# The causal mask of the first query block: a matmul with an identity, or an add inside the masked maximum

## The chip, the cores and the metric

The kernel runs on one core of a Trainium2 chip. The metric is the device time in microseconds (us) of one execution. Three runs of the kernel before took 554.1, 554.99 and 555.74 us; the median is 554.99 us. The engines are called PE (TensorE: matmuls; PEld is its weight load), DVE (VectorE), ACT (ScalarE), POOL (GpSimd) and SP (SyncE, which issues most DMAs).

## The reference, cut to what matters

The program mixes two branches by a gate: an attention with a compressive memory over four segments of 512 tokens, 16 heads of 28, and a feed-forward network (448 to 1792 to 448 with SiLU).

```python
for s in range(N):                       # 4 segments, L = 512
    qs, ks, vs = q[:, :, s], k[:, :, s], v[:, :, s]
    logits = einsum("bhqd,bhkd->bhqk", qs, ks) * scale + mask      # mask: -1e9 above the diagonal
    p = softmax(logits)
    a_dot = einsum("bhqk,bhkd->bhqd", p, vs)
    num = einsum("bhld,bhde->bhle", phi(qs), M)
    den = einsum("bhld,bhd->bhl", phi(qs), z)[..., None] + 1e-6
    o = g * num / den + (1 - g) * a_dot
    M, z = M + einsum("bhld,bhle->bhde", phi(ks), vs), z + phi(ks).sum(l)
a = concat(o) @ wo
b = silu(x @ w1) @ w2
out = gate * a + (1 - gate) * b          # gate = sigmoid(sum(x * gate_w))
```

What the change touches is the maximum of each row of `logits`, which the softmax needs before the exponentials, under the causal mask.

## The kernel before, in words

**Precision.** Operands of matmuls are split in two fp16 halves, so most products are three passes; a product over 448 rows is 11 matmuls (L616).

**Work.** There are 16 groups `t`: 4 segments times 4 groups of 4 heads. For each group the kernel projects q and k, retrieves from the memory, and then:

- `maxima(t, o)` computes the row maxima. Scores are made for query blocks of 128 rows (`i` = 0 to 3) against 128 x (i+1) keys, in PSUM banks of the ring "sc" (three banks of 512 columns). The plan is: block 0 for four heads in one bank, block 1 for two heads at a time, blocks 2 and 3 for one head at a time. For `i > 0` DVE makes one pass per head: it adds the mask from the tile `MK` and takes the maximum (L731, a masked maximum with an accumulator that is read out into `mx`). `MK` is 512 columns wide, zero but for its last 128, which hold the causal triangle; `MK[:, L - n:]` serves every block. For `i == 0` one matmul first writes the triangle into the bank for all four heads (L717: identity times `maskb`, 512 columns), the four score matmuls add to it (L721), and one plain reduce of 512 columns gives four maxima (L726). Then the maxima are lifted (L739), transposed on PE (L741), split in halves (L743, L745) and sent as two more rows of the group's q operand by two small DMAs.
- `attention(t)` makes the transposed scores with these rows (L1293), exponentials on ACT (L1298), the causal zeros on POOL (L1301, L1304), halves on ACT and POOL (L1310, L1314), the product with v (L1327), a reduce on DVE (L1335), the scaling on POOL (L1343, L1344) and a store.
- `ffn(i, ...)` runs the feed-forward network in two passes over its 14 blocks; its first product is L616, its second L1197, and tanh, products and halves between them lie on ACT and DVE (L1174 to L1180). It fills PE between the steps of the attention.
- `last_part` runs in the last stage: it loads the attention's output `o` and the memory's share, adds them on POOL (L627), makes halves (L633, L583), transposes by DMA (L641), multiplies by wo (L616 with `oT`), and adds the feed-forward part (L1404, L1408).

**The order.** Nothing of this order is written out by hand. Every step is a task with a modelled cost, dependencies, buffers of rings and a priority, and `Sched.run` (L221) lists them: at each turn it takes the engine whose best task can start first by the modelled costs; among tasks of an engine that can start at the same moment the lower priority number goes first, and for PE `matmuls` (L210) adds PRICE times a measure of uncovered weight loads. Each engine, and the DMA queue of SP, then executes its tasks in that order. So any changed cost or priority can redraw the whole order. The cost of a DVE task is 0.07 us + 0.00104 us per column (L328). Constants at the head of the file (L34 to L91) set the priorities: MAXO how early maxima come, FLO and FHI the span of the feed-forward's priorities in the first pass, WOP and WOT how far output projections, their loads and their features stand from the feed-forward work of their block, PVP and LOP those of the product with v and of the low halves, SLACK when an elementwise step goes to the other engine.

**The start.** PE begins with matmuls on the zeroed tile `maskb`: 8 in one task (L797, WARM) and MORE more in a chain at the low priority 200 (L802), which fill the time until the first weights and x have come. When the last of them is done, POOL writes the triangle into `maskb` (L818), as it has before into `MK` (L816); both selects are in `MKS`, for which every group's maxima wait.

```python
for _ in range(MORE):
    END1.append(pe(half(L), lambda: nc.tensor.matmul(
        wb.v, maskb, maskb[:, None, :].to_broadcast([128, 4, 128]), start=True, stop=True),
        END1[-1], uses=[wb], prio=200))
t_wb = END1[-1]
```

Of the kernel before, what the change touches and what calls it, by code (L numbers as in the profile page):

```python
# [14 lines left out]
OP = mybir.AluOpType  # L15
# [18 lines left out]
NA = 5  # L34
COLD = 5.0
WARM = 8
MORE = 34
HPRIO = -62.95
BANKS = {"mm": 3, "sc": 3, "cc": 2}
FREE = FB - 1  # L40
PASSES = [list(range(0, 10)), list(range(10, FB))]
# [3 lines left out]
DOWN = 2.0 ** -19  # L45
TINY = 2.0 ** -40
FIT = 2.0 ** -15
WOT = 71.68
TUS = 1.6
TLAT = 4.0  # L50
SLACK = -0.05
LOP = 28.11
LATE = 0.06
FIRST = 114.09
WPRIO = 110.43
MAXO = 61.39
FULL = 0.111
LOCK = 0.06
RB = "cc"
MP = 24.55  # L60
VF = 0.36
VA = 7.02
VS = 10.8
NV = 8
XH0 = -20.97
WQS = -0.58
VH = -12.56
XS0 = -18.17
VC = -7.5
OT1 = -4.94  # L70
XS = 8.61
QS = -10.12
KS1 = 3.46
SS = -19.24


def VP(o, k):
    return o + VA + VS * k if o or k > VF else -1.0 + 0.1 * k


PRICE = 135.04
PVRUNS = [((1, 0), 1)]
PVP = 21.83
FLO = -2.23
FHI = 720.62
WOP = 1.45
SZ = 35.49
SZSTEP = 1.68
XPRIO = -25.01
WBP = 7.24  # L90
XLEAD = 146.82  # L91


# [179 lines left out]
def infini_mix(ctx: ExitStack, tc: tile.TileContext, x, wq, wk, wv, wo, beta, w1, w2, out):  # L273
# [40 lines left out]
    def half(cols, n=1):  # L314
        return [(0.0025 + cols * 0.000418, 0.027)] * n

    def pe(seq, fn, *deps, **k):
        t = sch.add("PE", sum(max(a[0], b[1]) for a, b in zip(seq, seq[1:])) + seq[-1][0], fn, deps, **k)
        t.lead, t.tail = seq[0][1], seq[-1][0]
        return t  # L320
# [376 lines left out]
    def maxima(t, o):  # L697
# [12 lines left out]
        for q, (i, hs) in enumerate(plan):  # L710
            ps = Buf(BK["sc"])
            n = 128 * (i + 1)
            p0 = o - MAXO + 40 * q / len(plan)

            def go(i=i, hs=hs, ps=ps, n=n):
                if i == 0:
                    nc.tensor.matmul(ps.v, identb, maskb[:, None, :].to_broadcast([128, 4, 128]), start=True,  # L717
                                     stop=False, skip_group_check=True)
                for j, hh in enumerate(hs):
                    u = j * n  # L720
                    nc.tensor.matmul(ps.v[:, u:u + n], rg.v[:KS, 0, hh, i * 128:(i + 1) * 128], rg.v[:KS, 1, hh, :n],  # L721
                                     start=(i > 0), stop=(i > 0 or j == 3), skip_group_check=(i == 0))

            def red(i=i, hs=hs, ps=ps, n=n):
                if i == 0:
                    nc.vector.tensor_reduce(mx.v[:, :, 0], ps.v.rearrange("p (h n) -> p h n", h=4), axis=AX.X,  # L726
                                            op=OP.max)
                    return
                for j, hh in enumerate(hs):
                    r = ps.v[:, j * n:(j + 1) * n]  # L730
                    nc.vector.tensor_tensor_reduce(r, r, MK[:, L - n:], 1.0, NEG, OP.add, OP.max,  # L731
                                                   mx.v[:, hh, i:i + 1])
            m = pe((half(512) if i == 0 else []) + half(n, len(hs)), go, *rs, *MKS, takes=[ps], uses=[rg], prio=p0)
            reds.append(dve(len(hs) * (n + 45) - 45 if i else 512, red, m, *reds[:1], takes=[] if reds else [mx], uses=[ps, mx],
                            prio=p0))
        pt, mh = Buf(BK["sc"]), Buf(C["mhl2"])
        p0 = o - 20
# [14 lines left out]
    def project():  # L752
# [58 lines left out]
        def guards():  # L811
            for j in guard:
# [2 lines left out]
        t_mz = dve(L, lambda: nc.vector.memset(MK, 0.0), prio=-50)  # L815
        MKS.append(pool(128, lambda: nc.gpsimd.affine_select(MK[:, 384:], MK[:, 384:], [[-1, 128]], OP.is_ge, NEG,  # L816
                                                             base=0, channel_multiplier=1), t_mz, prio=-50))
        MKS.append(pool(128, lambda: nc.gpsimd.affine_select(maskb, maskb, [[-1, 128]], OP.is_ge, NEG, base=0,  # L818
                                                             channel_multiplier=1), t_wb, t_mb, prio=-50))
        ONE.append(dma(16e3, lambda: start(onescr.rearrange("a h (b n) -> (a h b) n", b=16), ones[:, :32]), t_on,  # L820
                       prio=50))

# [660 lines left out]
```

## Time and profile before

| | before |
|---|---|
| median of 3 runs | 554.99 us |
| the profiled execution's own time | 555.17 us |
| its span, first to last instruction | 553.1 us |
| PE busy | 540.6 us (98%) |
| DVE busy | 404.9 us (73%) |
| ACT busy | 392.6 us (71%) |
| POOL busy | 345.7 us (63%) |
| DMA, mean over the span | 143 GB/s |

How to read it: a time of the profile is inside the span; the own time of the execution is 2.07 us longer. Matmuls are pipelined, so a matmul's duration overlaps the next one's, and the distance of starts tells what one costs a busy PE. Rows of groups give the line, engine, operation, what is written and read (buffer numbers left out), count, busy time, mean ns of one, and the idle time of the engine just before with what ended it. Rows of the timeline give start, length, engine, line, operation and count, and in brackets an idle time before. Idle time of an engine that is not the bound costs nothing.

### The profile page before, as it was taken

The page shows a single profiled execution, that of the slowest core. Times are in us where ns is not written, and L with a number is a line of the kernel's source. Part 1 is how long each engine was busy: PE and PEld are TensorE (multiplying, and loading weights), DVE is VectorE, ACT ScalarE, POOL GpSimd, SP SyncE. Part 2 cuts the span into 40 slices and gives each one's busy share as a digit, 9 for nine tenths or more (in the row PEclk, how much of TensorE's full clock was granted, in tenths as well). Part 3 has the DMA queues.
Part 4 walks back from the last instruction along what each step waited for, and adds up shares of the span by engine and source line. Part 5 has one row for each costly group of instructions (what it writes and reads, how often), then busy time and mean ns, then how long its engine had stood idle before and what let it go on. Part 6 is the DMA issues. An engine that isn't in the chain of part 4 may idle for free.

```text
span 553.1 us, 11692 instructions
## 1 busy us (share of the span) xinstructions
PE 540.6 (98%) x4084; PEld 301.8 (55%) x4084; DVE 404.9 (73%) x1009; ACT 392.6 (71%) x694; POOL 345.7 (63%) x556
## 2 busy tenths in 40 slices
PE   8899999999999999999999999999999999999987
PEld 3445556656544555555565555555556554555534
DVE  5996999978779964788666889757895149653472
ACT  5887978866557978899787798878997897401140
POOL 3115535756424888899989898888978995212210
PEclk9999999999999999999999999999999999999999
DMA  8687557554567424224232243665200213698872
GB/s 305 202 263 229 189 172 213 162 165 143 178 181 202 122 74 146 71 70 106 70 115 84 70 125 102 136 147 162 55 24 32 85 35 95 219 230 234 224 187 84
DMA packets 78059, 78.94 MB, mean 143 GB/s; under 512 B 44040, under 2 KB 67720, under 8 KB 78000
## 3 DMA queue, kind: packets, MB, share of 16 engines
q1 hardware_dynamic: 77424, 77.21, 48.7%
q10 hardware_dynamic: 576, 0.99, 0.6%
q8 instruction: 32, 0.52, 0.4%
q14 instruction: 27, 0.22, 0.1%
HBM read 48.41 MB, written 26.09 MB: 135 GB/s over the span
## 4 chain that ended last, share of the span: by engine, by line
PE 72%; DVE 11%; DMA 8%; POOL 3%; SPq 2%; issue 2%; ACT 2%; DVEq 0%; POOLq 0%; ACTq 0%
PE mm L616 22%; PE mm L1197 15%; PE sc L1293 6%; PE sc L721 6%; PE cc L1327 6%; PE sc L616 5%; PE cc L1197 4%; PE cc L616 4%; DMA ol<-o_scr 3%; DMA rawf<-in_w_dram 3%; DVE sc L731 2%; DVE xh L583 1%; DMA xraw<-in_x_dram 1%; POOL ol L627 1%; SPq L641 1%
## 5 line engine op out<-in xcount | busy, mean ns | idle before, releaser
L1314 POOL TENSOR_TENSOR phl<-pf,phl 128x384 f16<-128x384 f32 (+1 forms) x192 | 189.7, 1010 | 21.3 <-ACT phl L1310 21.2
L731 DVE CUSTOM_DVE_ANT_0 sc<-sc,mk 128x384 f32<-128x384 f32 (+1 forms) x192 | 105.3, 571 | 30.1 <-PE sc L721 28.6
L1298 ACT ACTIVATE pf<-sc,es 128x512 f32<-128x512 f32 (+1 forms) x192 | 109.5, 618 | 25.1 <-PE sc L1293 22.8
L1197 PE MATMUL mm<-wb,ghl 128*128 128x448 f16 (+1 forms) x516 | 112.6, 348 | 0.0
L616 PE MATMUL mm<-xh,wa 128*128 128x512 f16 x429 | 106.3, 378 | 0.0
L1197 PEld LDWEIGHTS <-ghl 128*128 128x128 f16 x684 | 64.8, 97 | 54.4 <-DVE ghl L1180 2.2
L1310 ACT ACTIVATE phl<-pf 128x1280 f16<-128x1280 f32 x64 | 81.3, 1272 | 11.7 <-POOL pf L1304 11.5
L616 PEld LDWEIGHTS <-wa 128*128 128x128 f16 x572 | 54.4, 97 | 56.5 <-issue 2.6
L1293 PE MATMUL sc<-ring 86*128 86x512 f16 (+3 forms) x256 | 58.6, 299 | 1.3 <-DVE mx L726 1.0
L721 PE MATMUL sc<-ring 84*128 84x128 f16 (+3 forms) x256 | 57.3, 299 | 0.1
L1327 PEld LDWEIGHTS <-phl 128*128 128x128 f16 x1280 | 42.0, 96 | 10.4
L1335 DVE TENSOR_REDUCE oraw<-cc 128x116 f32<-128x232 f32 x64 | 25.3, 395 | 30.0 <-PE cc L1327 29.9
L627 POOL TENSOR_TENSOR ol<-ol,ml 128x448 f32<-128x448 f32 x12 | 13.6, 1133 | 48.5 <-DMA ol<-o_scr 36.3
L1327 PE MATMUL cc<-vg,phl 128*128 128x29 f16 (+1 forms) x1280 | 43.6, 182 | 0.0
L616 PE MATMUL mm<-xh,wqs 128*128 128x512 f16 x176 | 43.1, 379 | 0.0
L616 PE MATMUL mm<-xh,wks 128*128 128x512 f16 x176 | 42.1, 379 | 0.0
L1197 PE MATMUL cc<-wb,ghl 128*128 128x448 f16 x168 | 37.9, 352 | 2.0 <-DVE ghl L1180 1.3
L616 PE MATMUL sc<-wvs,xh 128*128 128x450 f16 x176 | 37.5, 353 | 1.6 <-DVE wvs L583 1.1
L633 ACT ACTIVATE oh<-ol,os 128x448 f16<-128x448 f32 x16 | 10.7, 666 | 39.8 <-POOL ol L627 39.8
L616 PE MATMUL cc<-xh,wa 128*128 128x512 f16 x143 | 37.2, 378 | 0.8 <-DVE amr L1055 0.8
L1293 PEld LDWEIGHTS <-ring 86*128 86x128 f16 x256 | 24.2, 97 | 21.7 <-issue 0.3
L616 PE MATMUL sc<-wos,oT 128*128 128x448 f16 x176 | 35.7, 352 | 0.0
(183 smaller groups left out, 933.7 us busy)
## 6 DMA issues: line engine op xcount, KB each, us to landing
rawf<-in_w_dram SPq DMA_DIRECT2D x26, 256.0 KB
rawf<-in_w_dram SPq DMA_DIRECT2D x28, 224.0 KB
v_scr<-vt SPq DMA_DIRECT2D x16, 232.0 KB
vg<-v_scr SPq DMA_DIRECT2D x16, 232.0 KB
xraw<-in_x_dram SPq DMA_DIRECT2D x14, 256.0 KB
q_scr<-stg SPq DMA_DIRECT2D x16, 224.0 KB
ring<-q_scr SPq DMA_DIRECT2D x16, 224.0 KB
k_scr<-stg SPq DMA_DIRECT2D x16, 224.0 KB
```

The lines of the kernel that those rows point to most:

```text
L616: nc.tensor.matmul(ps(), *p[i], start=(i == 0), stop=(i == n - 1))
L627: d = pool(530, lambda: nc.gpsimd.tensor_add(b.v, b.v, m.v), d, e, uses=[b, m], **k)
L633: hi = copy(D + 110, lambda: nc.scalar.activation(half2.v[:, :D], ol.v, AF.Copy, scale=sc), *ready, takes=[half2], uses=[ol], prio=prio)
L721: nc.tensor.matmul(ps.v[:, u:u + n], rg.v[:KS, 0, hh, i * 128:(i + 1) * 128], rg.v[:KS, 1, hh, :n], start=(i > 0), stop=(i > 0 or j == 3), ...
L731: nc.vector.tensor_tensor_reduce(r, r, MK[:, L - n:], 1.0, NEG, OP.add, OP.max, mx.v[:, hh, i:i + 1])
L1197: nc.tensor.matmul(ps.v[:, lo:hi], g.v[:, y, sl], w.v[:, z, lo:hi], start=(j == 0 and i == 0), stop=(j == len(fs) - 1 and i == 2))
L1293: nc.tensor.matmul(ps.v[:, e:e + w], rg.v[:KK, 1, hh, j * 128:(j + 1) * 128], rg.v[:KK, 0, hh, j * 128:], start=True, stop=True)
L1298: ex.append(sact(e, lambda b=b, ps=ps, pf=pf, e=e: nc.scalar.activation(pf.v[:, b, :e], ps.v[:, :e], AF.Exp, scale=es[:, s:s + 1]), m, *ex ...
L1310: hi = copy(1280, lambda hl=hl, flat=flat: nc.scalar.activation(hl.v[:, 0], flat(), AF.Copy), *mk, takes=[hl], uses=[pf], prio=p0 + 2)
L1314: low = pool(w - u + 22, lambda hl=hl, flat=flat, u=u, w=w: nc.gpsimd.tensor_sub(hl.v[:, 1, u:w], flat()[:, u:w], hl.v[:, 0, u:w]), low, u ...
L1327: nc.tensor.matmul(p[:, i, :2 - z], hl.v[:, z, u:u + 128], vg.v[:, j, hh, :2 - z], start=(z == zs[0] and i == 0), stop=(z == zs[-1] and j ...
L1335: nc.vector.tensor_reduce(orw.v[:, hh], p, axis=AX.X, op=OP.add)
```

## The change

For the first query block of each group the mask matmul (L717) and the reduce over four heads (L726) go. The block is treated like the others: four score matmuls, each with a start of its own, and four masked maxima of 128 columns, one a head, that add the triangle from the last 128 columns of `MK`. The planner's cost of this DVE task goes from 512 columns to 4 x 173 - 45 + 140 = 787, and that of the PE task loses one matmul of 512 columns. The triangle is no longer written into `maskb`, and `MKS` has one entry. MORE goes from 34 to 20 warm-up matmuls. Some thirty constants have other values, so that the planner draws another order.

```diff
@@ -34,8 +34,8 @@
-MORE = 34
-HPRIO = -62.95
+MORE = 20
+HPRIO = -74.28
@@ -45,49 +45,49 @@
-WOT = 71.68
+WOT = 48.81
...
-SLACK = -0.05
-LOP = 28.11
-LATE = 0.06
-FIRST = 114.09
-WPRIO = 110.43
+SLACK = 0.36
+LOP = 26.49
+LATE = 0.04
+FIRST = 108.19
+WPRIO = 114.09
...
-MP = 24.55
-VF = 0.36
-VA = 7.02
-VS = 10.8
+MP = 25.11
+VF = 0.19
+VA = 6.82
+VS = 10.57
...
-XH0 = -20.97
-WQS = -0.58
-VH = -12.56
-XS0 = -18.17
+XH0 = -22.77
+WQS = -0.68
+VH = -11.04
+XS0 = 0.52
...
-OT1 = -4.94
-XS = 8.61
-QS = -10.12
-KS1 = 3.46
-SS = -19.24
+OT1 = 11.56
+XS = 8.23
+QS = -1.8
+KS1 = 2.1
+SS = -19.38
...
-PRICE = 135.04
+PRICE = 93.57
...
-PVP = 21.83
-FLO = -2.23
-FHI = 720.62
-WOP = 1.45
-SZ = 35.49
-SZSTEP = 1.68
-XPRIO = -25.01
-WBP = 7.24
+PVP = 37.11
+FLO = -5.65
+FHI = 804.0
+WOP = -92.54
+SZ = 37.12
+SZSTEP = 1.71
+XPRIO = -17.35
+WBP = 7.18
@@ -713,25 +713,18 @@
             def go(i=i, hs=hs, ps=ps, n=n):
-                if i == 0:
-                    nc.tensor.matmul(ps.v, identb, maskb[:, None, :].to_broadcast([128, 4, 128]), start=True,
-                                     stop=False, skip_group_check=True)
                 for j, hh in enumerate(hs):
                     u = j * n
                     nc.tensor.matmul(ps.v[:, u:u + n], rg.v[:KS, 0, hh, i * 128:(i + 1) * 128], rg.v[:KS, 1, hh, :n],
-                                     start=(i > 0), stop=(i > 0 or j == 3), skip_group_check=(i == 0))
+                                     start=True, stop=True)
 
             def red(i=i, hs=hs, ps=ps, n=n):
-                if i == 0:
-                    nc.vector.tensor_reduce(mx.v[:, :, 0], ps.v.rearrange("p (h n) -> p h n", h=4), axis=AX.X,
-                                            op=OP.max)
-                    return
                 for j, hh in enumerate(hs):
                     r = ps.v[:, j * n:(j + 1) * n]
                     nc.vector.tensor_tensor_reduce(r, r, MK[:, L - n:], 1.0, NEG, OP.add, OP.max,
                                                    mx.v[:, hh, i:i + 1])
-            m = pe((half(512) if i == 0 else []) + half(n, len(hs)), go, *rs, *MKS, takes=[ps], uses=[rg], prio=p0)
-            reds.append(dve(len(hs) * (n + 45) - 45 if i else 512, red, m, *reds[:1], takes=[] if reds else [mx], uses=[ps, mx],
+            m = pe(half(n, len(hs)), go, *rs, *MKS, takes=[ps], uses=[rg], prio=p0)
+            reds.append(dve(len(hs) * (n + 45) - 45 + (140 if i == 0 else 0), red, m, *reds[:1], takes=[] if reds else [mx], uses=[ps, mx],
                             prio=p0))
@@ -815,8 +808,6 @@
-        MKS.append(pool(128, lambda: nc.gpsimd.affine_select(maskb, maskb, [[-1, 128]], OP.is_ge, NEG, base=0,
-                                                             channel_multiplier=1), t_wb, t_mb, prio=-50))
```

## The prediction

> **What bounds the kernel now.** I read the head of the page first, then the busy time by stage, then what TensorE (PE) waited for.
>
> ```profile
> span 553.1 us, 11692 instructions
> PE 540.6 (98%) x4084; PEld 301.8 (55%) x4084; DVE 404.9 (73%) x1009; ACT 392.6 (71%) x694; POOL 345.7 (63%) x556
> ...
> PE 72%; DVE 11%; DMA 8%; POOL 3%; SPq 2%; issue 2%; ACT 2%; DVEq 0%; POOLq 0%; ACTq 0%
> ```
>
> PE is busy for 98% of the span and makes 72% of the chain that ended last. A high PE share can still hide other limits, so the stages come next. Columns: stretch, its length, then busy time of each engine (instructions).
>
> ```profile
> 0.00:14.56 14.56, 12.23 (x48) 5.18 (x49) 8.43 (x35) 8.30 (x22) 4.98 (x27) 1.00 0.89 309
> 14.56:58.88 44.32, 42.96 (x231) 22.23 (x232) 39.28 (x84) 34.87 (x81) 12.94 (x43) 1.00 0.76 237
> 58.88:166.28 107.40, 105.56 (x624) 61.77 (x623) 92.57 (x200) 76.70 (x166) 53.53 (x117) 1.00 0.58 170
> 166.28:427.90 261.62, 260.21 (x2400) 149.59 (x2398) 199.35 (x579) 220.65 (x347) 224.91 (x312) 1.00 0.38 101
> 427.90:470.00 42.10, 42.10 (x373) 23.03 (x372) 21.82 (x41) 34.65 (x55) 34.64 (x45) 1.00 0.22 68
> 470.00:549.46 79.46, 77.49 (x414) 40.00 (x412) 42.65 (x72) 17.38 (x28) 14.71 (x13) 1.00 0.73 203
> 549.46:553.10 3.64, 0.01 (x1) 0.00 (x0) 0.81 (x2) 0.00 (x0) 0.00 (x0) 1.00 0.20 63
> ```
>
> The first stretch is warm-up, the last is the output's way home. In the five between, PE stands idle 1.36 + 1.84 + 1.41 + 0.00 + 1.97 = 6.58 us of 534.90. The maxima run in the third and fourth, where DVE (VectorE) is busy 92.57 of 107.40 us (86%) and 199.35 of 261.62 us (76%): PE is the bound, and DVE has room, less of it early. What PE waited for, in total, times and longest:
>
> ```profile
> PE cc L1197 <- DVE ghl L1180: 1.3, 2, 0.9
> PE sc L616 <- DVE wvs L583: 1.1, 1, 1.1
> PE sc L1293 <- DVE mx L726: 1.0, 1, 1.0
> ...
> PE sc L951 <- DVE mx L731: 0.3, 1, 0.3
> PE sc L1293 <- DVE mx L731: 0.2, 1, 0.2
> ```
>
> Only 1.0 + 0.3 + 0.2 = 1.5 us of waits come from the maxima holding a PSUM bank of the ring "sc".
>
> **The change, part by part.** The profiled execution took 555.17 us, its span is 553.1 us, so 2.07 us lie around it; it stands 0.18 us above the median of 554.99 us. The sum is made against 555.17.
>
> *The mask matmul goes.* Sixteen groups, one matmul of 512 columns each:
>
> ```profile
> L717 PE MATMUL sc<-maskb,identb x16: 377/379/379, 58.9 to 412.2; 128*128 128x512 bf16 x16
> ```
>
> ```profile
> 412.18 0.38 PE L717 MATMUL sc<-maskb,identb 128*128 128x512 bf16 x1
> 412.40 0.39 PE L721 MATMUL sc<-ring 84*128 84x128 f16 x4
> ```
>
> Its 379 ns duration overlaps its neighbour. What it costs a busy PE is the distance to the next start, 412.40 − 412.18 = 0.22 us. The warm-up row below with eight 512-column matmuls in 1.89 us gives the same more finely: (1.89 − 0.38) / 7 = 0.216 us. 16 × 0.216 = 3.46 us, and each lies in a stage where PE hardly idles (idle 1.84 and 1.41 us in the third and fourth), so nearly all of it is on the path: −3.46 us, with −3.2 at the low end (idle share of about 1% and 0.2 us for a group that meets a wait). The four products of each group stay, with a start of their own.
>
> *DVE's work grows.* Before, one reduce of 512 columns for four heads; after, four masked maxima of 128 columns, each with a read of the accumulator. No row shows the 128-column form; its sisters do.
>
> ```profile
> L731 DVE CUSTOM_DVE_ANT_0 sc<-sc,mk 128x384 f32<-128x384 f32 (+1 forms) x192 | 105.3, 571 | 30.1 <-PE sc L721 28.6
> ...
> L731 DVE DVE_READ_ACCUMULATOR2_ANT mx<- 128x1 f32 x192 | 26.9, 140 | 0.0
> ...
> L726 DVE TENSOR_REDUCE mx<-sc 128x4 f32<-128x512 f32 x16 | 10.8, 676 | 0.4 <-PE sc L721 0.4
> ```
>
> ```profile
> 300.92 2.42 DVE L739 TENSOR_SCALAR mx<-mx,lift 128x16 f32<-128x16 f32 x1
> ...
> 304.16 0.68 DVE L726 TENSOR_REDUCE mx<-sc 128x4 f32<-128x512 f32 x1
> 304.75 0.24 DVE L1339 RECIPROCAL rl<-oraw 128x16 f32<-128x16 f32 x1
> ...
> 306.58 0.43 DVE L731 CUSTOM_DVE_ANT_0 sc<-sc,mk 128x256 f32<-128x256 f32 x1
> ...
> 307.11 0.43 DVE L731 CUSTOM_DVE_ANT_0 sc<-sc,mk 128x256 f32<-128x256 f32 x1
> ...
> 307.46 0.27 DVE L745 SCALAR_TENSOR_TENSOR mhl<-sc,mhl 16x128 f16<-16x128 f32 x1
> ...
> 311.41 0.69 DVE L731 CUSTOM_DVE_ANT_0 sc<-sc,mk 128x512 f32<-128x512 f32 x1
> ...
> 312.02 0.40 DVE L1335 TENSOR_REDUCE oraw<-cc 128x116 f32<-128x232 f32 x1
> ...
> 327.37 0.56 DVE L731 CUSTOM_DVE_ANT_0 sc<-sc,mk 128x384 f32<-128x384 f32 x1
> ...
> 327.85 0.69 DVE L1180 SCALAR_TENSOR_TENSOR ghl<-mm,ghl 128x512 f16<-128x512 f32 x1
> ```
>
> By starts, a masked maximum with another kind behind it takes 0.35 us at 256 columns, 0.48 at 384 and 0.61 at 512: 0.13 us for each 128, so 0.22 at 128. With a second masked maximum right behind, the read of the accumulator shows: 307.11 − 306.58 = 0.53, which is 0.18 more. Four in a row: 3 × (0.22 + 0.18) + 0.22 = 1.42 us, against 304.75 − 304.16 = 0.59 us now. That is +0.83 us a group, +13.3 us of DVE in all (bounds 4 × 0.22 and 4 × 0.53, so +0.3 to +1.5 a group, +5 to +24). The planner books 0.07 + 0.00104 × 787 = 0.89 us, so each group runs 0.53 us later than the written order assumes.
>
> How much reaches PE? Behind the group in DVE's queue stand the FFN's L1176 and L1180 and the copies of the projections, for which PE's banks wait; in the bank ring the third taker after it waits (the score matmuls of L1293). The lower end is 0: DVE sat idle 28.6 us before L731 waiting for PE, and such pauses take up 0.83 us. The upper end is all 13.3. Of all maxima work, 105.3 + 26.9 + 10.8 = 143.0 us, 1.5 us came back as PE waits: 1.0%, so 0.14 us. Of L726 alone it was 1.0 of 10.8, 9%, so 1.2 us, but that one wait fell where L726 had to stand behind the unusual L739 of 2.42 us above. I take +0.4, nearer the first.
>
> [...]
>
> *Fourteen fewer warm-up matmuls* (MORE 34 to 20), and the select on maskb goes:
>
> ```profile
> 1.04 3.60 PE L797 MATMUL mm<-maskb 128*128 128x512 bf16 x8 [1.04 <-DVE maskb L793]
> 4.43 3.38 PE L802 MATMUL mm<-maskb 128*128 128x512 bf16 x13
> ...
> 7.78 2.97 PE L802 MATMUL mm<-maskb 128*128 128x512 bf16 x13
> 11.70 0.39 PE L460 MATMUL cc<-sums,ones 128*128 128x5 f32 x2 [0.95 <-DVE sums L459]
> 11.94 1.89 PE L802 MATMUL mm<-maskb 128*128 128x512 bf16 x8
> ...
> 14.56 0.94 PE L616 MATMUL sc<-wvs,xh 128*128 128x450 f16 x4 [0.24 <-DVE xh L596]
> ```
>
> The last warm-up ends at 13.83 and the first real matmul at 14.56 waited for DVE's xh: 14 × 0.216 = 3.0 us of PE go, and none was on the path. Value 0, no gain possible. But their cover goes too: twenty would end near 7.78 + 7 × 0.216 + 0.16 = 9.5 us, and until 14.56 PE would have only pairs of L460. If the clock falls back, the next stretch starts as the span did: 3.39 / 8 = 0.42 us a matmul, for the eight and some two more (the first row of 13 is 0.41 us longer than the second), 4.2 us at half speed, 2.1 us lost, of which the wait of 1.1 us for wvs hides a part: bounds 0 and +2.1. The granted clock in the stages reads 1.00 even where the starts are 0.42 us apart, so that column decides nothing. I take 0: the L460 pair at 11.70 parts the time into gaps of 2.2 us (9.5 to 11.70) and 2.5 us (12.09 to 14.56), and the one idle gap that the head shows now, 0.95 us, slowed nothing after it.
>
> [...]
>
> The maskb select is one POOL instruction in a stretch where POOL is busy 4.98 of 14.56 us: 0, and no one in the real work waited for it.
>
> *The redrawn order.* No DMA is added or taken away; SP's, ACT's and POOL's queues hold the same steps in another order. The largest shift is WOP (1.45 to −92.54): the 16 output projections and the loads and transposes before them move behind FFN work in the last stage, 92 of 1000 priority units over some 80 us, about 7 us later for the products and twice that for the loads. What covers them is FFN work; without it the last projection (2.24 us in the row under rival two) would stand after everything. Bounds: at best the 6.58 us of PE idle go, at worst as much is added (the only size that this trace offers). Nothing tells the sign: 0.
>
> Sum: 555.17 − 3.46 + 0.4 + 0 + 0 = 552.1; against the median, less 0.18, 551.9 us (−0.56%). A change below 0.3% (1.7 us) is about what a measurement of this kernel cannot tell from none.
>
> **Rivals.**
>
> 1. *The longer hold of the bank decides* (slower). Place: the ring of three "sc" banks between 166 and 428 us. For: each group overruns its plan by 0.53 us and holds its bank 0.83 us longer. Against: only 1.5 us of such waits now. It is slower once 3.46 / 13.3 = 26% of the extra DVE time reaches PE; at a half, 6.65 − 3.46: 558.2 us.
> 2. *The saving is given back*: the attention's pace is set by POOL (224.91 of 261.62 us, 86%), and after it the chain of o loads and transposes sets the end. For:
>
> ```profile
> 538.06 1.22 SPq L641 DMA_TRANSPOSE oT<-oh  x1
> ```
>
> ```profile
> 544.92 2.24 PE L616 MATMUL sc<-wos,oT 128*128 128x448 f16 x11
> ```
>
>    The last transpose is issued only 11.4 us before PE's end at 549.46, and the projection that uses it starts at 544.92. Against: POOL has 36.7 us of idle, and PE none between 427.90 and 470. It gives 555.0.
> 3. *The clock falls back in the head*: 551.9 + 1.0 to 2.1, middle 553.5. For: 5 us with hardly a matmul. Against: L460 at 11.70 parts it.
> 4. *The redrawn order opens waits as large as the present ones*: 551.9 + 6.58 = 558.5. For: every stage is reordered and the plan books the new group short. Against: the same rules (bank rings, PRICE, due times) still write it.
>
> **How the numbers follow.** Saving reaches the end: 0.62 (its own range 548.6, with half of the idle gone, to 553.3). Rival one 0.14, two 0.06, three 0.06, four 0.12. Faster by over 0.3%: 0.62. Within 0.3%: rivals two and three, 0.12 (553.5 is −0.27%). Slower: 0.26. The range from 548.5 to 558.2 leaves out some 0.05 below and, with about half of rivals one and four, 0.13 above.
>
> **What would show it.** Right: no L717; PE busy shorter by 3.46 + 3.0 us; 64 masked maxima of 128 columns at about 0.3 us each, DVE busy up by some 13 us net; PE waits on mx below 2 us; 512-column matmuls 0.216 us apart after 14.56. Wrong: PE waits for mx of 4 us or more (rival one); idle of PE after 470 well above 2 us (two, or WOP); 0.42 us steps after 14 us (three); new waits elsewhere (four).

## The result, and the profile after

The changed kernel took 559.64 us (median of six runs, 558.98 to 561.36), beside 555.37 us for the kernel before on the same chip (553.68 to 556.2). The ratio is 1.0086, with a 95% interval from 1.0063 to 1.0109: slower, where the prediction said 551.9 us and faster, and above its range. The profiled span went from 553.1 to 557.3 us. In the experiments below one execution stands far off, 1443.48 us in the kernel before with the lift on ScalarE, and is not in its ratio.

In the kernel after, the lines have moved: the score matmuls of the maxima L721 are L718, the masked maxima L731 are L724, the lift L739 is L732, the transpose of the maxima L741 is L734, the attention's scores L1293 are L1284, POOL's halves L1314 are L1305. (In the experiments' kernels they are again a few lines off.) First the head of the page after, with the shares of the chain that ended last:

```profile
span 557.3 us, 11766 instructions
...
PE 538.3 (97%) x4054; PEld 298.4 (54%) x4054; DVE 417.7 (75%) x1123; ACT 390.2 (70%) x691; POOL 348.4 (63%) x556
...
PE 77%; DVE 9%; DMA 6%; ACT 5%; issue 2%; SPq 0%; POOL 0%; DVEq 0%; ACTq 0%; POOLq 0%
```

PE is busy for 2.3 us less and yet the span is 4.2 us longer. DVE is busy for 12.8 us more. The stages of the kernel after, in the same columns as before (stretch, its length, busy time of each engine, then the granted clock, the DMA share and GB/s):

```profile
0.00:14.67 14.67, 8.95 (x35) 3.93 (x35) 8.33 (x35) 8.21 (x22) 4.59 (x26) 0.98 0.88 308
14.67:51.73 37.06, 36.71 (x187) 17.79 (x187) 35.18 (x77) 29.06 (x66) 8.06 (x24) 0.96 0.73 228
51.73:168.25 116.52, 114.07 (x668) 65.47 (x667) 97.94 (x212) 80.16 (x175) 63.61 (x139) 1.00 0.59 174
168.25:430.00 261.75, 255.78 (x2365) 146.17 (x2364) 211.88 (x685) 219.85 (x348) 223.88 (x310) 1.00 0.36 100
430.00:470.00 40.00, 40.00 (x364) 22.16 (x363) 16.38 (x34) 30.88 (x49) 33.10 (x45) 1.00 0.28 84
470.00:552.82 82.82, 82.82 (x442) 42.91 (x439) 46.45 (x80) 21.98 (x36) 15.14 (x13) 1.00 0.70 189
552.82:557.30 4.48, 0.00 (x0) 0.00 (x0) 1.49 (x3) 0.00 (x0) 0.00 (x0) 0.94 0.30 102
```

PE's idle time in the five stretches between head and tail is 0.35 + 2.45 + 5.97 + 0 + 0 = 8.77 us, against 6.58 before. It has moved: the last stage lost its 1.97 us, and the stretch from 168 to 430 us, where the maxima and the attention run, went from 1.41 to 5.97. The head is 0.11 us longer, the tail 4.48 instead of 3.64 us.

The idle rows understate it. A 512-column matmul lasts 0.38 us where the next can start after 0.22, so a stop of up to 0.16 us leaves no idle time. Taking PE's real matmuls one by one, from the first on, as the distance of starts less the columns at full clock (0.22 us for 512), the time that is not streaming grew from 15.8 to 22.5 us (+6.7), while the streaming shrank from 518.85 to 515.30 (−3.55, the sixteen mask matmuls). With head and tail that is the span: −3.55 + 6.7 + 0.11 + 0.84 = +4.1 us. (The levels hang on what one takes for a column's time, the differences hardly.) Of the 6.7 us the attention's scores (L1284) have +4.3, the transposes of the maxima (L734) +2.7, L616 +1.6 (a stretch of half clock, below, less a wait of 1.1 us for wvs that is gone), and the feed-forward's second product (L1188) −2.55.

What PE waited for in the kernel after, in total, times and longest:

```profile
PE sc L1284 <- DVE mx L724: 3.6, 4, 2.7
PE cc L460 <- DVE sums L459: 2.6, 1, 2.6
PE cc L460 <- ACT junk L438: 2.1, 2, 1.8
PE sc L734 <- DVE mx L732: 1.8, 2, 1.6
...
PE sc L942 <- DVE mx L724: 0.3, 1, 0.3
```

The waits for the maxima and the lift are 3.6 + 1.8 + 0.3 = 5.7 us, where the three rows of before gave 1.5. The prediction had set 4 us as the sign of its first rival. The two waits of L460 lie in the head, ahead of the first real matmul.

The new groups and the lift in the kernel after, shapes kept apart (columns: count, busy time, mean ns):

```profile
L724 DVE DVE_READ_ACCUMULATOR2_ANT mx<- 128x1 f32 x256 | 36.2, 141 | 0.0
...
L724 DVE CUSTOM_DVE_ANT_0 sc<-sc,mk 128x128 f32<-128x128 f32 x64 | 19.2, 300 | 3.1 <-PE sc L718 1.3
...
L732 DVE TENSOR_SCALAR mx<-mx,lift 128x16 f32<-128x16 f32 x16 | 10.0, 623 | 0.2
```

The largest wait, 2.71 us, in the timeline after:

```profile
289.60 1.77 POOL L1305 TENSOR_TENSOR phl<-pf,phl 128x384 f16<-128x384 f32 x2
...
290.60 3.28 DVE L732 TENSOR_SCALAR mx<-mx,lift 128x16 f32<-128x16 f32 x1
...
291.82 2.02 POOL L1305 TENSOR_TENSOR phl<-pf,phl 128x512 f16<-128x512 f32 x2
...
293.79 0.28 DVE L724 CUSTOM_DVE_ANT_0 sc<-sc,mk 128x128 f32<-128x128 f32 x1
...
294.17 0.30 DVE L724 CUSTOM_DVE_ANT_0 sc<-sc,mk 128x128 f32<-128x128 f32 x1
...
294.96 0.30 DVE L724 CUSTOM_DVE_ANT_0 sc<-sc,mk 128x128 f32<-128x128 f32 x1
...
295.17 0.39 DVE L1326 TENSOR_REDUCE oraw<-cc 128x116 f32<-128x232 f32 x1
...
295.37 0.27 PE L1284 MATMUL sc<-ring 86*128 86x256 f16 x1 [2.71 <-DVE mx L724]
```

Read it from the bottom. PE's L1284 waits for a bank that the next group's block 0 holds. That block's four maxima start at 293.79 and run in a row to 295.17: 1.38 us. They start late because the lift of the group before stands ahead of them in DVE's queue, for 3.28 us, though its tile has 128 x 16 numbers and its shortest took 0.22 us. It ends at 293.88, when POOL's pair of 2.02 us ends (293.84). Before, the lift of 2.42 us was quoted as unusual; behind it stood two other steps (0.60 and 0.31 us by starts) and then the reduce of 0.59 us, and PE waited 1.03 us.

Two things are mixed here: longer work, and an order in which it falls badly. Each can be run without the other.

### The profile page after: what moved, and what is told of

It reads as the page before. It is cut to its first block, busy times and chain, and to the rows that moved or that the text cites. A ratio compares the mean times of both kernels' runs of the same rounds, so it can differ in the third digit from the quotient of the medians.

```text
span 557.3 us, 11766 instructions
## 1 busy us (share of the span) xinstructions
PE 538.3 (97%) x4054; PEld 298.4 (54%) x4054; DVE 417.7 (75%) x1123; ACT 390.2 (70%) x691; POOL 348.4 (63%) x556
## 4 chain that ended last, share of the span: by engine, by line
PE 77%; DVE 9%; DMA 6%; ACT 5%; issue 2%; SPq 0%; POOL 0%; DVEq 0%; ACTq 0%; POOLq 0%
PE mm L616 23%; PE mm L1188 16%; PE sc L616 9%; PE sc L1284 6%; PE cc L1318 6%; PE cc L1188 6%; PE sc L718 5%; PE cc L616 5%; DMA rawf<-in_w_dram 4%; DVE sc L724 3%; ACT rawf L448 1%; DMA xraw<-in_x_dram 1%; PE cc L1040 1%; DVE mx L724 1%; DVE xh L583 1%
## 5 line engine op out<-in xcount | busy, mean ns | idle before, releaser
L1305 POOL TENSOR_TENSOR phl<-pf,phl 128x384 f16<-128x384 f32 (+1 forms) x192 | 189.1, 1007 | 19.8 <-ACT phl L1301 19.6
L724 DVE CUSTOM_DVE_ANT_0 sc<-sc,mk 128x128 f32<-128x128 f32 (+3 forms) x256 | 123.5, 506 | 29.9 <-PE sc L718 25.4
L1188 PE MATMUL mm<-wb,ghl 128*128 128x448 f16 (+1 forms) x516 | 111.8, 348 | 0.0
L616 PE MATMUL mm<-xh,wa 128*128 128x512 f16 x429 | 108.2, 378 | 0.0
L1188 PEld LDWEIGHTS <-ghl 128*128 128x128 f16 x684 | 64.4, 97 | 51.2 <-issue 0.3
L1301 ACT ACTIVATE phl<-pf 128x1280 f16<-128x1280 f32 x64 | 81.2, 1273 | 12.3 <-POOL pf L1295 12.2
L616 PEld LDWEIGHTS <-wa 128*128 128x128 f16 x572 | 53.8, 97 | 55.0 <-issue 3.2
L1284 PE MATMUL sc<-ring 86*128 86x512 f16 (+3 forms) x256 | 59.7, 299 | 4.0 <-DVE mx L724 3.6
L718 PE MATMUL sc<-ring 84*128 84x128 f16 (+3 forms) x256 | 57.0, 299 | 0.3 <-DVE vt L973 0.2
L616 PE MATMUL mm<-xh,wks 128*128 128x512 f16 x176 | 42.6, 380 | 0.3 <-ACT pp L918 0.3
L616 PE MATMUL mm<-xh,wqs 128*128 128x512 f16 x176 | 42.4, 379 | 0.4 <-DVE wqs L583 0.4
L1165 ACT ACTIVATE th<-mm,ths 128x512 f32<-128x512 f32 x39 | 26.7, 687 | 20.9 <-PE mm L616 20.8
L616 PE MATMUL sc<-wvs,xh 128*128 128x450 f16 x176 | 38.8, 363 | 0.1
L616 PE MATMUL cc<-xh,wa 128*128 128x512 f16 x143 | 36.3, 378 | 1.5 <-DVE amr L1046 1.5
L1188 PE MATMUL cc<-wb,ghl 128*128 128x448 f16 x168 | 37.5, 352 | 0.0
L724 DVE DVE_READ_ACCUMULATOR2_ANT mx<- 128x1 f32 x256 | 36.2, 141 | 0.0
L1284 PEld LDWEIGHTS <-ring 86*128 86x128 f16 x256 | 23.8, 97 | 22.6 <-issue 1.4
```

The costliest lines, as they stand in the source:

```text
L616: nc.tensor.matmul(ps(), *p[i], start=(i == 0), stop=(i == n - 1))
L1165: e1 = sact(L, lambda ps=ps, th=th: nc.scalar.activation(th.v, ps.v, AF.Tanh, scale=ths[:, s:s + 1]), m, takes=[th], uses=[ps], prio=p0)
L1188: nc.tensor.matmul(ps.v[:, lo:hi], g.v[:, y, sl], w.v[:, z, lo:hi], start=(j == 0 and i == 0), stop=(j == len(fs) - 1 and i == 2))
L1284: nc.tensor.matmul(ps.v[:, e:e + w], rg.v[:KK, 1, hh, j * 128:(j + 1) * 128], rg.v[:KK, 0, hh, j * 128:], start=True, stop=True)
L1301: hi = copy(1280, lambda hl=hl, flat=flat: nc.scalar.activation(hl.v[:, 0], flat(), AF.Copy), *mk, takes=[hl], uses=[pf], prio=p0 + 2)
L1305: low = pool(w - u + 22, lambda hl=hl, flat=flat, u=u, w=w: nc.gpsimd.tensor_sub(hl.v[:, 1, u:w], flat()[:, u:w], hl.v[:, 0, u:w]), low, u ...
```

## The experiments

All ratios are against the kernel before on the same chip, with 95% intervals; 0.3% is about what these comparisons tell apart. "Frozen order" means that the planner is given the costs it had, so that every queue keeps its order and only what a step issues is changed.

### The new order with the old work, and the old order with the new work

The first puts the mask matmul, the reduce and the select back into the kernel after, in frozen order:

```diff
+                if i == 0:
+                    nc.tensor.matmul(ps.v, identb, maskb[:, None, :].to_broadcast([128, 4, 128]), start=True, ...
...
+                if i == 0:
+                    nc.vector.tensor_reduce(mx.v[:, :, 0], ps.v.rearrange("p (h n) -> p h n", h=4), axis=AX.X,
+                                            op=OP.max)
+                    return
```

> The order of the changed kernel in all queues, with the old work put back: mask matmul and one reduce per first block (and the select on maskb). 20 warm-up matmuls, so the slow clock at 14 us stays. HOLD: the waits on mx that the change brought (7 to 8 us) go, the 3.5 us of mask matmuls come back: 555 to 556.5 us, ratio 1.000 to 1.002. ORDER: the waits stay and the matmuls come on top: 563 us, ratio 1.014.

Measured: 1.0015 [0.9993, 1.0036], 556.71 us. The redrawn order with the 20 warm-ups can't be told from the old one when the work is old.

The second takes the same lines out of the kernel before, in frozen order, 34 warm-ups kept:

> The order of every queue is that of the kernel before, to the instruction (the planner still books the mask matmul and one reduce); only the work is new: no mask matmul, four masked maxima per first block. MORE stays 34. Theory HOLD (the four maxima keep DVE and the bank longer, and PE waits): 3.5 us of matmuls go, some 7 us of waits of L1293 and L741 on mx come, so about 558.5 us, ratio 1.006. Theory ORDER (the redrawn order is what costs): the waits stay near 1.5 us, 552 us, ratio 0.994.

Measured: 1.0136 [1.0076, 1.0197], 562.16 us. PE's waits in this kernel:

```profile
PE sc L1286 <- DVE mx L724: 7.8, 14, 2.1
```

Where the plan knows nothing of the longer group, 14 of the 16 groups make PE wait, 0.6 us as a rule.

What follows: the work is what makes it slower, in either order. The granted clock does not explain it: its mean over the executions is 0.994 in the kernel after and 0.993 with the old work put back, and 0.998 with the new work in the old order, beside 0.999 of the kernel before. From the two pairs the share of the DVE time that reached the end can be worked out. By starts a group of four maxima takes 1.38 us and the reduce took 0.59, so DVE got 16 × 0.79 = 12.6 us more. In the new order the work costs (1.0086 − 1.0015) × 555.4 = 3.9 us net (±1.7 us from the two intervals), and as PE streams 3.55 us less, 7.5 us came back: 59% of 12.6 (46 to 73%). In the old order 0.0136 × 555.4 = 7.6, and 3.55 more: 11.1 us, 88% (62% and up).

### DVE's time alone

To see that it is DVE's time and not, say, the missing matmul's place, the kernel before issues its reduce twice in each group, in frozen order; the mask matmul stays. The result is the same, and the group holds DVE and its bank longer, so these two are not parted here.

```diff
                 if i == 0:
+                    nc.vector.tensor_reduce(mx.v[:, :, 0], ps.v.rearrange("p (h n) -> p h n", h=4), axis=AX.X,
+                                            op=OP.max)
                     nc.vector.tensor_reduce(mx.v[:, :, 0], ps.v.rearrange("p (h n) -> p h n", h=4), axis=AX.X,
                                             op=OP.max)
```

> The kernel before, same order, mask matmul kept, but the reduce of each first block is issued twice, which adds 0.6 us of DVE to each group and nothing to PE. HOLD: PE waits on mx grow by most of what the change brought, +4 to +6 us, ratio 1.007 to 1.011. ORDER: DVE's pauses take it up, +0 to +0.5 us, ratio 1.000 to 1.001.

Measured: 1.0086 [1.0057, 1.0116], 560.27 us, that is +4.8 us. What DVE got shows in the first group of its timeline:

```profile
64.75 0.68 DVE L726 TENSOR_REDUCE mx<-sc 128x4 f32<-128x512 f32 x1
65.46 0.69 DVE L728 TENSOR_REDUCE mx<-sc 128x4 f32<-128x512 f32 x1
66.07 0.63 DVE L1057 TENSOR_REDUCE amr<-cc 128x232 f32<-128x464 f32 x1
```

By starts the two take 1.32 us where one took 0.60, so 0.72 us more in each group and 16 × 0.72 = 11.5 us in all: 42% of it came out (28 to 56%). Time not streaming went from 15.8 to 20.5 us, nearly all of the loss. Waits of PE and of its weight loads (PEld):

```profile
PEld L1295 <- DVE mx L728: 6.7, 14, 1.0
...
PE sc L1295 <- DVE mx L728: 1.2, 5, 0.5
...
PE sc L743 <- DVE mx L741: 0.8, 2, 0.6
```

The named waits of the matmuls are only a part (1.2 + 0.8 against 1.0 before): the rest shows as starts drawn apart. In 14 of the 16 groups the weight load of the attention's scores waits for the second reduce, where in the kernel before none waited for the one. DVE is busy for three quarters of the span, and still two fifths of what it is given more comes out at the end.

### The head: 34 warm-ups back, or 20 in the kernel before

```diff
-MORE = 20
+MORE = 34
```

> The changed kernel with 34 warm-up matmuls, all else in the same order. CLOCK (3.4 us at half speed from 14.3 us on cost 1.7 us): the clock record is 1.000 and the time 557.9 us, ratio 1.0055. If that loss is hidden by waits that follow in the head: 559.6 us, ratio 1.0086.

Measured: 1.0085 [1.006, 1.011], 559.91 us: no difference from the kernel after. The other way round, in the kernel before the last 14 of the 34 are planned but not issued:

```diff
-        for _ in range(MORE):
-            END1.append(pe(half(L), lambda: nc.tensor.matmul(
-                wb.v, maskb, maskb[:, None, :].to_broadcast([128, 4, 128]), start=True, stop=True),
+        for k in range(MORE):
+            END1.append(pe(half(L), lambda k=k: nc.tensor.matmul(
+                wb.v, maskb, maskb[:, None, :].to_broadcast([128, 4, 128]), start=True, stop=True) if k < 20 else None,
```

> The kernel before in its own order with the last 14 warm-up matmuls left out. CLOCK: the record shows 3.4 us (or 6.8) at half speed from about 14 us on; the matmuls there run at 0.37 us a piece, and 0.4 to 1.7 us reach the end: ratio 1.001 to 1.003. If gaps of 2.2 and 2.5 us do not slow the clock: record 1.000 and ratio 1.000.

Measured: 1.0012 [0.999, 1.0034], 556.62 us. It can't be told from no change; a loss above some 1.9 us is excluded, all but the top of the 1.0 to 2.1 that the third rival gave is not. (In its profile the clock is at half from 12.48 to 19.31 us, 6.83 us, of which some 2 us lie ahead of the first real matmul.)

The mechanism of that rival did take place. The head in the timeline after (PE), and two stretches of it in windows:

```profile
7.59 1.67 PE L795 MATMUL mm<-maskb 128*128 128x512 bf16 x7
11.82 0.39 PE L460 MATMUL cc<-sums,ones 128*128 128x5 f32 x2 [2.56 <-DVE sums L459]
14.03 0.57 PE L460 MATMUL cc<-sums,ones 128*128 128x5 f32 x2 [1.82 <-ACT junk L438]
14.67 3.83 PE L616 MATMUL sc<-wvs,xh 128*128 128x450 f16 x12
```

```profile
14.08:17.49 3.41, 3.34 (x10) 1.61 (x11) 3.28 (x8) 3.41 (x10) 0.18 (x1) 0.50 0.83 294
17.49:20.00 2.51, 2.51 (x16) 1.39 (x15) 2.35 (x8) 0.27 (x3) 0.00 (x0) 1.00 0.74 225
```

From 14.08 to 17.49 the granted clock is 0.50, and the first real matmuls run at half speed: their starts are 374 ns apart, and 190 ns behind the stretch. The longest gap ahead of them is 2.56 us. In time it is worth no more than 3.41 / 2 = 1.7 us, and a part of that is time in which PE would have waited for wvs.

With the 34 back the fall in the head goes (the mean granted clock of that execution, 0.996, has room for one fall of 3.42 us and not for two), and another comes later in the same kernel, behind the 2.71 us wait for the maxima, which is the same there:

```profile
291.00:294.45 3.45, 0.85 (x14) 0.41 (x11) 3.35 (x10) 2.06 (x3) 2.04 (x3) 1.00 0.50 140
294.45:297.87 3.42, 3.31 (x10) 1.46 (x10) 0.85 (x5) 1.30 (x3) 2.59 (x5) 0.50 0.15 40
```

So the price of the fall can't be read from this pair of kernels; a cleaner pair stands below. The mean granted clock differs between executions of one kernel, which gives a second reading. Of the ten executions with the 34 back, the one with a mean granted clock of 1.000 took 557.62 us, the five at 0.996 took 558.26 to 560.02, and the four at 0.991 to 0.994 took 560.17 to 562.39. Beside the experiments the kernel before ran 84 times, 61 times at 0.999 or 1.000 and 23 times at 0.995 to 0.997; in each of the four sets the latter took longer in the mean, by 0.7 to 1.9 us. All six executions of the kernel after stand at 0.990 to 0.996. So a lower clock goes with some 1 to 2 us; whether the fall alone makes them, or a longer wait brings both, these numbers do not part.

### Booking the true cost

The planner booked 0.89 us for the four maxima where they take 1.38. With 651 extra columns in place of 140 it books 1.42, and draws an order of its own:

```diff
-dve(len(hs) * (n + 45) - 45 + (140 if i == 0 else 0), ...
+dve(len(hs) * (n + 45) - 45 + (651 if i == 0 else 0), ...
```

> The changed kernel, all its constants, but the planner books the four masked maxima at 1.41 us, as the trace shows them (1.39 us), in place of 0.89; so it draws another order that knows when the bank comes free. Theory UNBOOKED (PE waits because the written order reuses the bank as soon as the plan says it is free): the waits of L1284 and L734 on mx fall from 9.3 us to 3 or less, 553 to 555 us, ratio 0.997 to 1.000. Theory LOAD (DVE has too much to do around the groups, whatever the order): waits stay above 6 us, ratio 1.005 or more.

Measured: 1.0112 [1.0079, 1.0145], 561.54 us. PE's waits in it:

```profile
PE cc L616 <- DVE amr L1046: 3.4, 1, 3.4
...
PE sc L1284 <- DVE mx L724: 0.4, 2, 0.2
```

The waits for the maxima are gone (5.7 to 0.4 us; the 9.3 named beforehand is more than the matmuls' rows hold), and the time is no better: a wait of 1.5 us for another step of DVE (L1046) grew to 3.4. The same in the constants of before, once with the costs of the change and once with the true cost; both have the new work and 34 warm-ups, and no constant of the change:

> The kernel before with the edit alone: its own constants and 34 warm-up matmuls, the planner's costs of the change (0.89 us booked). UNBOOKED: like the changed kernel, 0.5 us a group too late, ratio 1.004 to 1.010. If the redrawn constants were the fault: 552 us, ratio 0.994.

Measured: 1.0073 [1.0046, 1.01], 559.66 us.

```profile
PE mm L1188 <- DVE y L1399: 2.4, 1, 2.4
PE cc L1040 <- DVE md L1014: 1.7, 1, 1.7
...
PE sc L1284 <- DVE mx L724: 0.4, 2, 0.2
```

> As the run of the edit alone, with the four maxima booked at 1.41 us. UNBOOKED: the full 3.5 us come through, 551.5 to 553.5 us, ratio 0.993 to 0.997. LOAD: no better than the run with 0.89 us booked.

Measured: 1.0147 [1.0107, 1.0187], 562.98 us.

```profile
PE cc L616 <- DVE ghl L1171: 3.8, 1, 3.8
PE sc L718 <- DVE vt L973: 2.0, 1, 2.0
```

In all three the plan makes room for the maxima, the longest lift is 0.98 us, and PE waits for other steps of DVE instead. So neither the bank that the maxima hold nor a long lift is the cause by itself. The reading that fits all five orders with the new work is that DVE's time is short at the moment when PE needs it, and that the bank is the place where it shows in two of them; that is argued, not shown. Each of these redrawn orders also differs in much else, so none of them alone measures a price. They have falls of the clock too, at 13.90 and 157.26 us in the first, at 157.50 us in the second and three times in the profile of the third, which is of its slowest execution (566.52 us; the other three took 562.73 to 563.02).

### The lift taken off DVE

The timeline put the lift of 3.28 us ahead of the largest wait. It can be done by ScalarE (ACT), as a copy with a bias: POOL writes the negative lift beside the lift, and the step keeps its place in the plan. First in the order of the kernel after:

```diff
+            by(lift[:, NSEG + s:NSEG + s + 1], u, -1.0)
...
-        f0 = dve(155, lambda: nc.vector.tensor_scalar(mx.v, mx.v, lift[:, s:s + 1], None, op0=OP.subtract), ...
+        f0 = dve(155, lambda: nc.scalar.activation(mx.v, mx.v, AF.Identity, bias=lift[:, NSEG + s:NSEG + s + 1]), ...
```

> The changed kernel in its own order, but the lift of the maxima (L732, 128x16) runs on ScalarE in place of VectorE. Theory PORT (this small VectorE operation stands behind GpSimd's long ones, up to 3.28 us, and the four maxima queue behind it): the waits of 2.7, 1.6 and 1.6 us go, 555 to 556 us, ratio 0.999 to 1.001. If only the four maxima's own length counts: 559 us, ratio 1.007.

Measured: 0.9991 [0.997, 1.0013], 555.61 us, 0.95% less than the kernel after. The waits for the maxima (first fence, PE's waits) are now of 0.6 us at most, and the lift (second fence, its group) takes 309 ns in the mean and 348 at most:

```profile
PE sc L1285 <- DVE mx L725: 1.5, 4, 0.6
```

```profile
L733 ACT ACTIVATE mx<-mx,lift 128x16 f32<-128x16 f32 x16 | 5.0, 309 | 0.0
```

The rival reading was that the lift is long because of what it reads and writes, not because DVE has it. So it was left on DVE and moved behind the transpose, where it works on 16 x 128 numbers in PSUM:

```diff
-        f0 = dve(155, lambda: nc.vector.tensor_scalar(mx.v, mx.v, lift[:, s:s + 1], None, op0=OP.subtract), *reds, EREADY[s],
+        f0 = dve(155, lambda: None, *reds, EREADY[s],
...
+        def top_half():
+            nc.vector.tensor_scalar(pt.v[:16, :128], pt.v[:16, :128], lift[:16, s:s + 1], None, op0=OP.subtract)
```

> The changed kernel in its own order; the lift stays on VectorE, but works after the transpose, in PSUM (16x128 in place of 128x16 in SBUF). VectorE keeps an instruction of 0.2 to 0.3 us per group. PORT (only an operation with its operands in SBUF stands behind GpSimd's): no lift longer than 0.4 us, the long waits on mx go as with the lift on ScalarE, 555 to 556 us, ratio 0.999 to 1.001. If it was VectorE's load that the move to ScalarE relieved: 557.5 us or more, ratio above 1.003.

Measured: 1.007 [1.0045, 1.0095], 560.21 us. Its lift is never long, 347 ns at most, but DVE now waits for PE's transpose ahead of it (its group, then PE's waits):

```profile
L738 DVE TENSOR_SCALAR sc<-sc,lift 16x128 f32<-16x128 f32 x16 | 5.4, 340 | 3.2 <-PE sc L734 3.2
```

```profile
PE sc L1288 <- DVE mx L724: 2.1, 6, 0.6
...
PE sc L718 <- DVE vt L977: 1.2, 1, 1.2
```

The long lifts went, and a new dependence took their place in the time. By what was expected beforehand, 1.003 or more speaks for DVE's load and against the stalled lift as what ScalarE relieved; with the new waits for the transpose in it (3.2 us of DVE's idle time), the run does not settle it. As a test of the lift it says that here, with POOL's work as before, the same operation on PSUM operands took 295 to 347 ns, where on SBUF operands it took 216 to 3282.

Then the kernel before, with its own order and work, and the lift on ScalarE:

> The kernel before, same order, lift on ScalarE. PORT: the one wait of 1.0 us behind the lift of 2.42 us goes, and the wait of the last stage is untouched: 554.3 us, ratio 0.998. If there is nothing to gain without the four maxima: 1.000.

Measured: 0.9957 [0.9934, 0.9979], 553.47 us, faster than both kernels. Time not streaming falls from 15.8 to 12.2 us: by 0.9 in the attention's scores and by 2.5 in the feed-forward's second product.

The new work in the old order, with the lift on ScalarE:

> The order of the kernel before, the new maxima, lift on ScalarE. There each group met a wait of about 0.6 us with no long lift near it. PORT alone would take off the waits of 2.3 and 1.0 us: 558.5 us, ratio 1.006, with ten or more waits of L1286 on mx left. If the lift was behind all of them: 553 us, ratio 0.996.

Measured: 1.0072 [1.0049, 1.0095], 560.24 us; the same edit is worth 0.64% here, though the two intervals overlap. PE's waits keep the 0.6 us of the longer group in 10 places:

```profile
PE sc L1287 <- DVE mx L725: 3.6, 10, 0.6
```

Last a clean pair in the new order, with the lift on ScalarE and 34 warm-ups, once with the new work and once with the old:

> The changed kernel in its own order with the lift on ScalarE and 34 warm-up matmuls. If the slow clock in the head costs its 1.7 us once the other waits are gone: 553.5 us, ratio 0.996; if waits in the head hide it: 555 us, ratio 0.999.

> The order of the changed kernel, 34 warm-up matmuls, lift on ScalarE, but mask matmul and one reduce per first block put back: the same kernel with the new maxima took ratio 0.9968. Theory LENGTH (the four maxima's own 0.8 us more per group still costs more PE time than the 3.5 us of matmuls that they save): ratio 0.992 to 0.995, faster with the old work. Theory PORT ALONE (with the lift out of the way the new maxima cost nothing): the old work is 3.5 us slower, ratio 1.003.

Measured: 0.9968 [0.9954, 0.9983] (554.6 us) with the new work, 0.999 [0.9972, 1.0008] (555.03 us) with the old. The intervals overlap slightly: the new work is the same or about 0.2% faster here.

What follows. With the lift off DVE, the share of the 12.6 us that comes back falls in the new order to (0.9968 − 0.999) × 555.4 = −1.2 us net, so 2.3 of 12.6: 18% (8 to 29%), where it was 59%. In the old order (1.0072 against 0.9957) it is 6.4 + 3.55 = 9.9 us, 79%, where it was 88%. So in the order drawn for the new work most of the loss needed both: the long group, and the lift on DVE. Whether the lift counts by its one long stall ahead of the group or by the 10.0 us that it takes of DVE in all is open. In an order that books the old reduce, the longer group is enough.

Against the same kernel with 20 warm-ups (0.9991), the first of the pair also prices the head: the 14 warm-ups are worth 0.23%, some 1.3 us, though the intervals overlap. The granted clocks agree: 0.997 to 1.000 with the 34, 0.989 to 0.997 with the 20.

## Why the prediction was wrong

**The mask matmul: right.** −3.46 us was predicted, PE's streaming fell by 3.55. PE's busy time fell by 2.3 and not by 3.46 + 3.0 us, since starts drawn apart by short stops or a half clock still count as busy (3.34 of the 3.41 us at half clock).

**DVE's added work: right in size.** Four in a row were put at 1.42 us and took 1.38; the 128-column pass was put at 0.3 us of duration and takes 300 ns; DVE's busy time was to rise by some 13 us and rose by 12.8.

**How much of it reaches PE: wrong, and this is the step that failed.** The sum has +0.4 for it, 3% of 13.3 us. The runs show 7.5 us, 59%, in the new order, 88% in the old, and 42% for the doubled reduce. The prediction took the share from waits that were there: 1.5 us of waits after 143.0 us of maxima, 1.0%, and 9% for L726 alone. That is a mean over work that the order already held; what counts is what the next microsecond does. The doubled reduce, which adds DVE time and moves nothing in any queue, lost 4.8 us of its 11.5. In an order that books the old reduce the overrun of 0.8 us a group makes PE wait 14 times of 16. The pauses of DVE ahead of the maxima, 28.6 us, did not take it up: 25.4 us of them are left in the kernel after and 28.2 in the old order with the new work. Why so large a share comes through is in part open: an overrun of the booking can't be all of it, since booking the true cost made no order faster.

**The row that was set aside.** The prediction saw the lift of 2.42 us and the wait that stood behind it, called it unusual, and took the nearer mean. It is one lift of 16, but no chance: it took 2.42 us again in the kernel before with 20 warm-ups, and the one of 3.28 us in the kernel after took 3.28 again with 34. In the kernel after the group that was made longer is what queues behind it. Without the lift on DVE the three kernels were 0.95% (the new order), 0.64% (its work in the old order) and 0.43% (the old order and work) faster; how much of that is the stall, and how much the load, is open.

**Rival one** had the direction, its sign (waits for mx of 4 us or more: 5.7) and its break-even at 26%; at the half it named 558.2 us, and 559.64 was measured. Its chance of 0.14 was the error, with the term it belongs to. Where it names the bank, the planning runs correct it: with the true cost booked the waits for the bank go to 0.4 us and the time stays.

**Rival two**, the saving given back in the last stage: it did not come. The last stage has no idle time any more (1.97 to 0.00 us), with the moved output projections; the tail is 0.84 us longer.

**Rival three**, the clock: the mechanism came, from 14.08 to 17.49 us, against the argument that the pair of L460 parts the gaps. That gaps of 2.2 and 2.5 us leave the clock alone was the author's estimate: no row of before shows it, and in the kernel after the fall came behind gaps of 2.56 and 1.82 us. Its price is bounded by 1.7 us at half speed; one pair puts it at some 1.3 us with overlapping intervals, in the other two it was not to be told from none, and among executions of one kernel a lower clock goes with some 1 to 2 us. The value 0 of the sum was probably a part of the error, and much the smaller one.

**Rival four**, the redrawn order: with the old work, and together with the 20 warm-ups, it measures 1.0015 [0.9993, 1.0036], so the value 0 was right in size. (WOP moves by 94 units, not the 92 that the prediction wrote; nothing hangs on it.) Its other half, that new waits open elsewhere, is what the three re-planned runs show.

The sum with the terms that the runs give, in the new order: −3.55 (mask matmuls) + 7.5 (DVE's work) + 0.8 (order and warm-ups, 0.0015 × 555.4) = +4.8 us, which is the ratio's 0.86%. It closes by construction, since the 7.5 was worked out from the same two ratios; the check from outside is the doubled reduce.

## What to carry to other kernels

Price added time on an engine that isn't the bound by what stands right behind it in its queue and in the ring of banks, not by the mean wait of such work so far: here 42 to 88% of the added time came through on an engine that was busy for only 75%, and 18% once another step had been taken off it in the order that was drawn for the new work. When an edit comes with a redrawn order, run the old work in the new order and the new work in the old: two runs parted the cause here. And look for small instructions with a maximum ten times their minimum: something may be queued behind the stall, and moving them to an engine with room gained more here than the change in hand.

## What the runs showed of the hardware that was not expected

**A tiny DVE instruction took up to 3.28 us while GpSimd worked.** The lift on 128 x 16 numbers in SBUF takes 0.22 us at the least, and one of 16 took ten times as long; before and after:

```profile
L739 DVE TENSOR_SCALAR mx<-mx,lift x16: 223/355/2422, 96.3 to 429.2; 128x16 f32<-128x16 f32 x16
```

```profile
L732 DVE TENSOR_SCALAR mx<-mx,lift x16: 216/408/3282, 95.4 to 432.0; 128x16 f32<-128x16 f32 x16
```

The numbers are minimum, median and maximum. The lift of 3282 ns ended 0.04 us after POOL's back-to-back L1305 (with a select of 0.51 us, L1295, between its rows). The next longest took 0.93 us before and 1.12 after. On PSUM operands the same operation had a mean of 340 ns over its 16 times, and on ScalarE of 309. The long one, from 290.60 to 293.88 us, spans several POOL instructions in a row (an L1305, L1295 and two more L1305, to 293.84 us), not one. That POOL's work is the cause is argued from where the long lift ends and from which operands have it, not shown.

**The clock fell behind gaps of PE of 1.82 to 2.71 us.** In the kernel after it was at 0.50 for 3.41 us behind gaps of 2.56 and 1.82 us with a pair of tiny matmuls between them, and in the kernel with the 34 warm-ups back for 3.42 us behind 3.45 us in which PE was busy for 0.85 and waited 2.71 at a stretch. In the old order with the new work it fell too, behind a wait of 2.1 us (windows of that kernel):

```profile
307.00:310.90 3.90, 1.76 (x10) 0.74 (x9) 3.29 (x12) 1.63 (x4) 1.27 (x4) 1.00 0.26 65
310.90:314.40 3.50, 3.50 (x31) 2.10 (x30) 2.15 (x9) 2.69 (x5) 3.50 (x6) 0.51 0.24 68
```

Yet the wait of 2.71 us in the kernel after, of the same length as in the kernel with 34 warm-ups, lost nothing: the granted clock reads 1.00 from 289.00 to 298.80 us. The falls of one execution, where it has several, lie on a grid. Two of them with the true cost booked, in the constants of the change:

```profile
13.90:17.31 3.41, 3.10 (x10) 1.24 (x10) 3.27 (x8) 3.41 (x11) 0.00 (x0) 0.50 0.88 315
157.26:160.67 3.41, 3.14 (x8) 1.17 (x8) 2.27 (x5) 0.00 (x0) 2.11 (x3) 0.50 0.25 72
```

They begin 143.36 us apart, 42 times 3.413; the three falls of the run with the true cost in the constants of before begin 85.33 and 317.44 us apart, 25 and 93 times. In the kernel after the next fall begins at 556.80 us, behind the last matmul and 158 times 3.413 us from 17.49. Counted on from 17.49 in such steps, a border falls in the kernel after at 293.97 us, in the middle of the 2.71 us that lost nothing. So by these runs the length of a gap alone does not tell whether the clock falls; that its place on the grid decides is argued, not shown.
